# Attention and a mixture of experts on one core: softmax sums rearranged between engines, the first expert layer set inside an attention, weights requested later

## The chip, the cores and the metric

The kernel runs on one core of a Trainium2 chip. The metric is the device time of one execution in microseconds (us). A core has five engines that run their own instruction streams side by side: TensorE (PE, matmuls and, as PEld, weight loads), VectorE (DVE), ScalarE (ACT), GpSimd (POOL) and SyncE (SP, which here only starts DMA transfers). They wait for one another through semaphores. Matmul results land in PSUM, everything else lives in SBUF.

## What is computed

Grouped-query attention (8 batches, 16 query heads, 4 key heads, 384 positions, head size 64), then a mixture of experts with two gates (4 groups of 4 experts, 1024 by 1024 layers) on its output. Cut to what matters:

```python
scores = scale * np.matmul(q, k.transpose(0, 1, 3, 2))
attn = np.exp(scores - max); attn = attn / (sum + 1e-09)
x = np.matmul(attn, v)                      # (3072, 1024)
g_idx = argmax(x @ w_group)                 # group, then expert in it
e_idx = argmax(xg @ w_expert[g])
h = np.maximum(x[mask_e] @ w1[g, e], 0.0)
out[tok_idx] = g_w * e_w * (h @ w2[g, e])
```

## The kernel before

A batch is worked in two stages. Its **attention** (`Attn.run`) goes through 24 chunks u: four key groups g of six chunks c. For chunk u it issues the scores of chunk u+2 on TensorE (L292), their exp on ScalarE into a tile `e` of 128 x 768 (L298), and then the P·V product of chunk u (`pv`, L311), fp32, into a PSUM tile of its group. `tail` (L320) folds the six `e` tiles of a group into one with five adds on VectorE (L318), and at the end of a group moves the PSUM tile into `xT`, on ScalarE (L345), for group 1 of batches 2 to 7 on VectorE (L343). Tiles `e` come from a pool of twelve. `reduce_keys` (L366) sums the four folded tiles over keys with a transposing reduction (L370), `sums` (L375) adds partitions by small matmuls (L379) and takes the reciprocal (L382), `normalise` (L384) spreads it by a transpose (L389) and multiplies (L394), `cast` (L396) writes bf16 `xb` on ScalarE.

The **block** of batch b (`block`, L659) comes after its attention and does the expert of batch b-1: `moe_h` (64 matmuls and four ReLUs), then the three output products `ffn_y` and `y_out`, and between them the closing sums, normalise and the gate of batch b: `gate_logits` (L409), `gate_tokens` (L434), `guess_mean` (L423, evacuated by L426), `guess_logits` (L439), `gate_softmax`. The gate also guesses from a mean of v which expert most tokens of the next batch will take; `pick` reads its number into a register of GpSimd, and `pick_w1`/`pick_w2` request that expert's weights, 2 MB each in bf16, on GpSimd's DMA queue. A loop at the end does experts that were not guessed; here it is entered zero times.

Batches 0 and 1 are the start: attention 0 runs alone, with the transposes of its queries and keys between chunks; attention 1 has the closing sums, normalise and gate of batch 0 as `inserts` between its chunks; block 1 then does the expert of batch 0. The order of all this is written out by hand: each engine executes its instructions in the order of the code. K and q of batch b+2 are requested on GpSimd's queue, v on SP's; SP then transposes k and q of batch b+1 by DMA (`trans_k`, `trans_q`, L127, L119), with all outputs behind it in the same queue.

Of the kernel before, what the change touches and what calls it, by code (L numbers as in the profile page):

```python
# [18 lines left out]
def kernel(  # L19
# [28 lines left out]
    NB = S // 32  # L48
    scale = 1.0 / (D ** 0.5)
# [208 lines left out]
    def first_scores():  # L258
        new_kT(0)
        new_qT(0)  # L260
        warm = ps_tile("o")
        for i in range(8):
            nc.tensor.matmul(out=warm[:, i % 2, :], lhsT=onesb[:, :P], rhs=onesb, start=True,
                             stop=True)
# [3 lines left out]
        first_k(0, "s", nc.vector)  # L268
        first_q(0, SC, "s", nc.scalar)
        first_q(SC, SC, "o", nc.vector)  # L270
        nc.gpsimd.tensor_copy(out=k16[0][:, NC:NK].rearrange("p c d -> p (c d)"), in_=k0f[:, 1])
# [3 lines left out]
    xT, xb, ess = {}, {}, {}  # L275

    class Attn:
        def __init__(self, b):
            self.b = b
            self.e, self.oT = {}, {}  # L280
            ess[b] = {}
# [35 lines left out]
        def add(self, u, v_):  # L317
            nc.vector.tensor_add(out=self.e[u], in0=self.e[u], in1=self.e[v_])  # L318

        def tail(self, u):  # L320
# [3 lines left out]
            if c == 0 and g:  # L324
                self.add(z - NC, z - NC + 2)
            elif c in (1, 3):
                self.add(u - 1, u)
            elif c >= 4:
                self.add(z + 2 * (c - 4), u)
            if c == NC - 1:  # L330
                ess[b][g] = self.e[z]
                if g == Hkv - 1:
                    self.add(z, z + 2)
# [17 lines left out]
        def run(self, inserts, nxt=None):  # L351
            for u in range(NU):
# [11 lines left out]
    red, inv = {}, {}  # L364

    def reduce_keys(b, gs):  # L366
        if b not in red:
            red[b] = gpool.tile([P, Hkv, 2, NB], F32, name="red")
        for g in gs:
            nc.vector.tensor_reduce(  # L370
                out=red[b][:, g].rearrange("p t j -> p (t j)"),
                in_=ess[b][g].rearrange("p t (j x) -> p (t j) x", x=32),
                axis=AX.X, op=ALU.add, apply_transpose=True)

    def sums(b, which):  # L375
        sm = ps_tile(which, [P, Hkv, KG, NB])
        for r in range(2):
            for t in range(2):
                nc.tensor.matmul(out=sm[t * D:(t + 1) * D, :, r, :], lhsT=half32[:, r, :],  # L379
                                 rhs=red[b][:, :, t, :], start=True, stop=True)  # L380
        inv[b] = gpool.tile([P, KQ, NB], F32, name="inv")
        nc.vector.reciprocal(out=inv[b], in_=sm.rearrange("p g r j -> p (g r) j"))  # L382

    def normalise(b, m):  # L384
        if b not in xb:
            xb[b] = xpool.tile([P, KQ, S], BF16, name="xb")
        ks = slice(2 * m, 2 * m + 2)
# [28 lines left out]
    def guess_mean(b, pt):  # L416
# [9 lines left out]
        nc.vector.tensor_copy(out=vm, in_=pm)  # L426
# [15 lines left out]
    def gate_softmax(b, glp, guess):  # L442
# [5 lines left out]
        nc.vector.tensor_copy(out=gl, in_=glp[:, lo:hi])  # L448
# [54 lines left out]
    def pick(b):  # L503
# [13 lines left out]
        ers[b] = nc.gpsimd.value_load(e_i[0:1, 0:1], min_val=0, max_val=NE - 1)  # L517
# [83 lines left out]
    state = {}
# [17 lines left out]

    GB = KG * SC  # L620
    at[0].run({
        0: [gate_matrix_b],
        1: [do(first_q, GB, GB, "x", nc.vector)],
        3: [index_constants],
        5: [do(first_k, 1, "x", nc.vector)],
        7: [do(first_q, 2 * GB, GB, "x", nc.scalar)],
        12: [do(first_q, 3 * GB, GB, "x", nc.scalar)],
        18: [first_guess],
        20: [first_pick],
    }, at[1])  # L630
    load_v(2)
    load_k(2)
    load_q(2)

    def first_gate():
        state["pt"] = ps_tile("x")
        state["vm"] = guess_mean(1, state["pt"])
        gate_logits(0, state["pt"])

    def first_softmax():  # L640
        glp = gate_rows(state["pt"])
        gate_tokens(0, glp)
        guess_logits(state["vm"], glp)
        weights[0] = gate_softmax(0, glp, True)
        pick(1)
        pick_w2(1)

    weights = {}
    ins = {0: [do(reduce_keys, 0, range(Hkv))], 4: [do(sums, 0, "x")]}
    for i in range(4):  # L650
        ins.setdefault(5 + 2 * i, []).append(do(normalise, 0, i))
        ins.setdefault(7 + 2 * i, []).append(do(cast, 0, i))
    ins.setdefault(4, []).append(do(before_attention, 1))
    ins.setdefault(13, []).append(first_gate)
    ins.setdefault(15, []).append(first_softmax)
    at[1].run(ins)
    nc.sync.dma_start(out=xb_dram[0], in_=xb[0])

    def block(b):  # L659
        last = b == B - 1  # L660
        f = b - 1
        if b + 2 < B:
            load_v(b + 2)
            load_k(b + 2)
            load_q(b + 2)
        moe_h(f, 0, "s")
        reduce_keys(b, range(Hkv))
        weights[f]()
        out_weights(f)
        moe_h(f, 2, "s")  # L670
        sums(b, "o")
        for m in range(4):
            normalise(b, m)
        moe_h(f, 4, "s")
        moe_h(f, 6, "s")
        cast(b, 0)
        cast(b, 1)
        if b == 1:
            pick_w1(1)
        moe_y(f, 0, "s")  # L680
        cast(b, 2)
        cast(b, 3)
        nc.sync.dma_start(out=xb_dram[b], in_=xb[b])
        y = ffn_y(w2s[f], hTs[f], 1, "s", (0,))
        gate_logits(b, ps_tile("o"))
        ffn_y(w2s[f], hTs[f], 1, "s", (1,), y)
        y_out(f, 1, y)
        pt = ps_tile("s")
        glp = gate_rows(pt)
        vm = None if last else guess_mean(b + 1, pt)  # L690
        gate_tokens(b, glp)
        if not last:
            guess_logits(vm, glp)
        y = ffn_y(w2s[f], hTs[f], 2, "o", (0,))
        if not last:
# [3 lines left out]
        if not last:  # L699
            pick(b + 1)  # L700
            pick_w1(b + 1)
        ffn_y(w2s[f], hTs[f], 2, "o", (1,), y)
        if not last:
            pick_w2(b + 1)
# [119 lines left out]
```

## Time and profile before

| | us |
|---|---|
| median of 3 runs (401.49 to 401.89) | 401.64 |
| the profiled execution | 401.64 |
| its span, first to last instruction | 399.7 |
| busy: TensorE / VectorE / ScalarE / GpSimd | 372.5 / 293.4 / 241.7 / 29.7 |
| mean granted TensorE clock | 0.983 |

The 1.9 us between the execution and its span lie outside what the profile shows. A busy share says how long an engine had an instruction in hand, not what the kernel waited for; that is read from the stretches, waits and timelines below. A period of the steady part (one attention and one block) is 45.3 us, and six of them make up most of the span.

### The profile page before, as it was taken

The page shows a single profiled execution, that of the slowest core. Times are in us where ns is not written, and L with a number is a line of the kernel's source. Part 1 is how long each engine was busy: PE and PEld are TensorE (multiplying, and loading weights), DVE is VectorE, ACT ScalarE, POOL GpSimd, SP SyncE. Part 2 cuts the span into 40 slices and gives each one's busy share as a digit, 9 for nine tenths or more (in the row PEclk, how much of TensorE's full clock was granted, in tenths as well). Part 3 has the DMA queues.
Part 4 walks back from the last instruction along what each step waited for, and adds up shares of the span by engine and source line. Part 5 has one row for each costly group of instructions (what it writes and reads, how often), then busy time and mean ns, then how long its engine had stood idle before and what let it go on. Part 6 is the DMA issues. An engine that isn't in the chain of part 4 may idle for free.

```text
span 399.7 us, 8883 instructions
## 1 busy us (share of the span) xinstructions
PE 372.5 (93%) x3631; PEld 196.3 (49%) x3631; DVE 293.4 (73%) x502; ACT 241.7 (60%) x328; POOL 29.7 (7%) x45
## 2 busy tenths in 40 slices
PE   7999567999999999999999999999999999999992
PEld 3455133554555455554555455554555445554541
DVE  4678994993799649993799749993799748994230
ACT  4599373634892659744893559735894549735220
POOL 5001100200100020000100020000100001000000
PEclk9999798999999999999999999999999999999998
DMA  8972999999999999999999999999999999954424
GB/s 200 221 104 55 213 212 155 207 241 250 246 190 197 168 266 226 196 196 225 280 174 197 167 250 214 199 197 237 270 144 177 175 271 176 214 100 134 104 65 95
DMA packets 71209, 76.02 MB, mean 190 GB/s; under 512 B 35928, under 2 KB 50264, under 8 KB 71168
## 3 DMA queue, kind: packets, MB, share of 16 engines
q0 software_dynamic: 26640, 41.03, 60.0%
q1 hardware_dynamic: 44176, 33.94, 40.1%
q8 instruction: 29, 0.48, 0.5%
q10 hardware_dynamic: 352, 0.48, 0.4%
q14 instruction: 12, 0.10, 0.1%
HBM read 89.21 MB, written 18.87 MB: 270 GB/s over the span
## 4 chain that ended last, share of the span: by engine, by line
PE 63%; DVE 15%; ACT 12%; issue 7%; DMA 1%; ACTq 0%; DVEq 0%
PE ps_s L549 19%; PE ps_s L558 14%; PE ps_o L311 10%; DVE e L318 9%; ACT e L298 9%; PE ps_o L558 8%; PE ps_s L292 5%; PE ps_o L409 3%; ACT xT L345 2%; DVE red L370 2%; PE ps_s L434 1%; PE ps_o L549 1%; DMA w<-in_moe_w_expert_dram 1%; ACT ot L573 1%; DVE rb L389 1%
## 5 line engine op out<-in xcount | busy, mean ns | idle before, releaser
L298 ACT ACTIVATE e<-ps_s 128x768 f32<-128x768 f32 x192 | 146.4, 824 | 36.0 <-PE ps_s L292 35.4
L311 PE MATMUL ps_o<-e,v_raw 64*64 64x384 f32 x1536 | 158.2, 494 | 2.3 <-DVE inv L382 1.5
L318 DVE TENSOR_TENSOR e<-e 128x768 f32<-128x768 f32 x160 | 145.0, 953 | 20.0 <-PE ps_o L311 9.6
L549 PE MATMUL ps_s<-xb,w 128*128 128x384 bf16 x480 | 80.8, 326 | 0.0
L311 PEld LDWEIGHTS ps_o<-e,v_raw 64*64 64x64 f32 x1536 | 62.7, 136 | 26.7 <-issue 15.3
L292 PE MATMUL ps_s<-qT,kT 64*64 64x384 bf16 x768 | 68.8, 338 | 4.8 <-ACT e L298 2.7
L549 PEld LDWEIGHTS <-w 128*128 128x128 bf16 x512 | 48.9, 98 | 36.0 <-issue 4.2
L551 ACT ACTIVATE hT<-ps_s 128x768 bf16<-128x768 f32 x30 | 24.3, 811 | 58.7 <-PE ps_s L549 58.7
L292 PEld LDWEIGHTS <-kT 64*64 64x64 bf16 x768 | 32.0, 107 | 54.2 <-issue 49.8
L558 PEld LDWEIGHTS <-hT 128*128 128x128 bf16 x384 | 36.0, 98 | 45.2 <-issue 5.4
L558 PE MATMUL ps_s<-w,hT 128*128 128x512 bf16 x248 | 56.4, 379 | 0.0
L558 PE MATMUL ps_o<-w,hT 128*128 128x512 bf16 x136 | 32.0, 379 | 0.0
L389 DVE STREAM_TRANSPOSE rb<-inv 128x768 f32<-128x768 f32 x32 | 31.3, 977 | 1.0
L370 DVE TRANSPOSE_TENSOR_REDUCE red<-e 128x24 f32<-128x768 f32 x32 | 28.4, 944 | 0.0
L394 DVE TENSOR_TENSOR xT<-xT,rb 128x768 f32<-128x768 f32 x28 | 26.8, 958 | 1.4
L577 ACT ACTIVATE ot<-ps_s,we 128x1024 f32<-128x1024 f32 x14 | 15.6, 1114 | 17.6 <-PE ps_s L558 17.6
L398 ACT CAST xb<-xT 128x768 bf16<-128x768 f32 x28 | 22.0, 829 | 1.7 <-DVE xT L394 1.7
L345 ACT COPY xT<-ps_o 128x768 f32<-128x768 f32 x22 | 17.5, 797 | 6.6 <-PE ps_o L311 6.6
L426 DVE CAST vm<-ps_s 128x4 bf16<-128x4 f32 x6 | 1.0, 162 | 27.7 <-PE ps_s L423 27.7
L492 POOL DMA_DIRECT2D w<-in_moe_w_dram x8 | 7.0, 879 | 114.3 <-PE ps_s L292 64.1
L409 PE MATMUL ps_o<-xT,wg 128*32 128x384 f32 x112 | 11.3, 524 | 4.4 <-DVE vm L426 4.4
L91 POOL DMA_DIRECT2D k<-in_k_dram x7 | 4.9, 706 | 92.1 <-DMA kT<-k 92.1
(114 smaller groups left out, 164.5 us busy)
## 6 DMA issues: line engine op xcount, KB each, us to landing
w<-in_moe_w_dram POOLq DMA_DIRECT2D x16, 2048.0 KB, 24.7
out_dram<-ot SPq DMA_DIRECT2D x42, 256.0 KB, 6.2
xb_scratch<-xb SPq DMA_DIRECT2D x8, 768.0 KB, 9.0
q_raw<-in_q_dram POOLq DMA_DIRECT2D x7, 768.0 KB, 15.5
v_raw<-in_v_dram SPq DMA_DIRECT2D x14, 384.0 KB, 7.9
out_dram<-ot SPq DMA_DIRECT2D x12, 128.0 KB, 2.3
k<-in_k_dram POOLq DMA_DIRECT2D x7, 192.0 KB, 11.9
w<-in_q_dram POOLq DMA_DIRECT2D x3, 192.0 KB, 7.2
```

Of the source, the lines that this page charges most:

```text
L292: nc.tensor.matmul(out=sT[r * H2:(r + 1) * H2, s, :S], lhsT=kT[b][s * D:(s + 1) * D, slot, ks], rhs=qT[b][s * D:(s + 1) * D, kq * SC:(kq + ...
L298: nc.scalar.activation(e.rearrange("p t (s x) -> p s t x", s=2), sT[:, :, :S].rearrange("p s (t x) -> p s t x", t=2), ACT.Exp, scale=scale)
L311: nc.tensor.matmul(out=oT[t * D:(t + 1) * D, r, :S], lhsT=vraw[b][r * H2:(r + 1) * H2, g, c * D:(c + 1) * D], rhs=self.e[u][r * H2:(r + 1) ...
L318: nc.vector.tensor_add(out=self.e[u], in0=self.e[u], in1=self.e[v_])
L345: nc.scalar.copy(out=dst, in_=src)
L370: nc.vector.tensor_reduce(out=red[b][:, g].rearrange("p t j -> p (t j)"), in_=ess[b][g].rearrange("p t (j x) -> p (t j) x", x=32), axis=AX ...
L389: nc.vector.transpose(out=rb.rearrange("p k (j x) -> p (k j) x", x=32), in_=inv[b][:, ks].rearrange("p k j -> p (k j)").unsqueeze(2).to_br ...
L394: nc.vector.tensor_mul(out=x, in0=x, in1=rb)
L409: nc.tensor.matmul(out=lg[32 * t:32 * t + 32, :S], lhsT=wg[:, kq, :], rhs=xT[b][:, kq, :], start=(jj == 0), stop=(jj == KQ // 4 - 1))
L549: nc.tensor.matmul(out=h[:, jj, :S], lhsT=w1[:, kq, (f0 + jj) * P:(f0 + jj + 1) * P], rhs=x[:, kq, :], start=(kq == 0), stop=(kq == KQ - 1))
L551: nc.scalar.activation(hT[:, f0:f0 + 2, :], h[:, :, :S], ACT.Relu)
L558: nc.tensor.matmul(out=y[:, nh, :], lhsT=hT[:, f, c * P:(c + 1) * P], rhs=w2[:, f, nh * HALF:(nh + 1) * HALF], start=(f == 0), stop=(f == ...
```

## The change

What it does, part by part:

- **Sums.** `tail` adds only two pairs of `e` tiles per group, now on GpSimd; VectorE reduces four tiles per group with the transposing reduction, into `red` with four entries per group, and `collect` adds the four. The 20 adds and 4 reductions of a batch on VectorE become 8 adds on GpSimd, 16 reductions and a small reduction on VectorE. For batches 0 and 1 reductions can be held back (`hold`) and issued later (`release`).
- **Copies.** For batches 2 to 7 VectorE moves all four PSUM tiles into `xT`; ScalarE no longer does.
- **Start.** Eight more matmuls of ones (`fill`) around the first scores; the gate matrix is built in chunks 4 and 5 of attention 0; constants move ahead.
- **Batch 0's closing work.** `sums` and `normalise` in two halves, the first within attention 0; the products of batch 0 on GpSimd.
- **Attention 1** stops after chunk 13: there stand `moe_h` of batch 0 and batch 0's gate, and half of batch 1's normalise; then chunks 14 to 23. Block 1 keeps the output products.
- **Weights.** `pick` only reads the register. The weights are requested at the start of the next block, after `transposed`, a one-column copy on GpSimd that waits for the query transposes of the following batch. K, q and v of batch b+2 follow them.
- **Gate.** `guess_mean` comes after `gate_tokens`, and `guess_logits` after half of the third output product.

```diff
+        def add(self, eng, u):
+            eng.tensor_add(out=self.e[u], in0=self.e[u], in1=self.e[u + 1])
+
+        def reduce(self, g, n, u):
...
+                nc.vector.tensor_reduce(
+                    out=reds[self.b][:, g, n].rearrange("p t j -> p (t j)"),
+                    in_=self.e[u].rearrange("p t (j x) -> p (t j) x", x=32),
+                    axis=AX.X, op=ALU.add, apply_transpose=True)
+            if self.held is None:
+                emit()
+            else:
+                self.held.append(emit)
...
-            if c == 0 and g:
-                self.add(z - NC, z - NC + 2)
-            elif c in (1, 3):
-                self.add(u - 1, u)
-            elif c >= 4:
-                self.add(z + 2 * (c - 4), u)
+            if c in (1, 3):
+                self.add(nc.gpsimd, u - 1)
+            if c >= 3:
+                self.reduce(g, c - 3, (z, z + 4, z + 5)[c - 3])
             if c == NC - 1:
+                self.reduce(g, NR - 1, z + 2)
...
-                if g == 1 and b > 1:
+                if b > 1:
                     nc.vector.tensor_copy(out=dst, in_=src)
...
+    def collect(b, g0, g1):
+        nc.vector.tensor_reduce(
+            out=rsum[b][:, g0:g1].rearrange("p g t j -> p g (t j)"),
+            in_=reds[b][:, g0:g1].rearrange("p g n t j -> p g (t j) n"), axis=AX.X, op=ALU.add)
...
+    def scale_x(b, m, rb, eng):
+        eng.tensor_mul(out=x, in0=x, in1=rb)
...
+    def transposed(b):
+        nc.gpsimd.tensor_copy(out=after, in_=qT[b][:, KQ * SC - 1, :1])
+    def first_fetch():
+        pick(0)
+        transposed(1)
+        pick_w1(0)
+        pick_w2(0)
...
+        14: [do(hold, a), first_guess],
+        16: [first_pick, do(collect, 0, 0, 2), a.release],
+        19: [do(sums, 0, 0, 2, "x"), do(spread0, 0), do(spread0, 1)],
+        21: [first_fetch],
     }, at[1])
+    collect(0, 2, Hkv)
+    loads(2)
+    a = at[1]
+    hold(a)
+    a.run(0, 14, {
+        0: [do(scale0, 0)],
+        2: [do(scale0, 1)],
+        4: [do(cast, 0, 0)],
+        6: [do(sums, 0, 2, Hkv, "x"), do(spread0, 2), do(spread0, 3), do(scale0, 2), do(scale0, 3),
+            do(cast, 0, 1), a.release, do(transposes, 2)],
+        11: [do(cast, 0, 2)],
+        13: [do(cast, 0, 3)],
+    })
+    moe_h(0, 0, "s")
+    pt = ps_tile("x")
+    gate_logits(0, pt)
+    moe_h(0, 2, "s")
+    glp = gate_rows(pt)
+    gate_tokens(0, glp)
+    vm = guess_mean(1, pt)
+    moe_h(0, 4, "s")
+    guess_logits(vm, glp)
+    collect(1, 0, 2)
+    weights[0] = gate_softmax(0, glp, True)
+    pick_index(1)
+    pick(1)
+    moe_h(0, 6, "s")
+    sums(1, 0, 2, "x")
+    normalise(1, 0)
+    normalise(1, 1)
...
+    a.run(14, NU, {})
     def block(b):
+        if not last:
+            transposed(b + 1)
+        pick_w1(b)
+        pick_w2(b)
         if b + 2 < B:
+            loads(b + 2)
```

Three places in the instruction order. First, VectorE in attention 1, from the last sums of batch 0 on. `e` tiles are written in place, `rb` is the spread reciprocal. Before:

```order
L318 TENSOR_TENSOR e<-e 128x768 x4
L370 TENSOR_REDUCE red<-e 128x24 x4
L318 TENSOR_TENSOR e<-e 128x768 x3
L382 RECIPROCAL inv<-ps_o_681 128x96
L318 TENSOR_TENSOR e<-e 128x768
L389 STREAM_TRANSPOSE rb<-inv 128x768
L394 TENSOR_TENSOR xT<-xT,rb 128x768
L318 TENSOR_TENSOR e<-e 128x768 x2
L389 STREAM_TRANSPOSE rb<-inv 128x768
L394 TENSOR_TENSOR xT<-xT,rb 128x768
L318 TENSOR_TENSOR e<-e 128x768
L389 STREAM_TRANSPOSE rb<-inv 128x768
```

Of the change:

```order
L413 STREAM_TRANSPOSE rb<-inv 128x768 x2
L336 TENSOR_REDUCE red<-e 128x24 x4
L395 TENSOR_REDUCE rsum<-red 128x48
L407 RECIPROCAL inv<-ps_o_733 128x48
L413 STREAM_TRANSPOSE rb<-inv 128x768 x2
L336 TENSOR_REDUCE red<-e 128x24 x8
L240 CAST vm<-ps_o_864 128x4
L395 TENSOR_REDUCE rsum<-red 128x48
```

The adds, and the products between the transposes, are gone from VectorE; reductions stand there, those of held tiles among them, and a reciprocal in two parts.

Second, GpSimd around the first request for weights (`w_568`, `w_608` are w1 of batch 0; `e_i` is its register's source; ISA rows work out the address). Before, from the cast of k on:

```order
L271 CAST w_84<-w_84 128x384
L517 TENSOR_LOAD e_i
L517 ISA x2
L492 ISA
L492 DMA w_568<-in_moe_w_dram 128x8x1024
L498 ISA
L498 DMA w_570<-in_moe_w_dram 128x8x1024
L91 DMA k_613<-in_k_dram 128x2x384
L96 DMA q_raw<-in_q_dram 128x8x384
```

Of the change, from the cast of k on:

```order
L281 CAST w_84<-w_84 128x384
L329 TENSOR_TENSOR e<-e 128x768 x7
L554 TENSOR_LOAD e_i
L554 ISA x2
L643 COPY after<-qT 128x1
L524 ISA
L524 DMA w_608<-in_moe_w_dram 128x8x1024
L530 ISA
L530 DMA w_610<-in_moe_w_dram 128x8x1024
L92 DMA k_642<-in_k_dram 128x2x384
L97 DMA q_raw<-in_q_dram 128x8x384
L423 TENSOR_TENSOR xT<-xT,rb 128x768
```

Seven more adds stand ahead of the register load, the marker copy behind it, and the products of batch 0 (L423) behind four requests.

Third, VectorE in a steady attention (batch 2), from the product `ot` on. Before:

```order
L574 TENSOR_SCALAR ot<-ps_o_1201,we 128x512
L318 TENSOR_TENSOR e<-e 128x768 x8
L343 COPY xT<-ps_o_1365 128x768
L318 TENSOR_TENSOR e<-e 128x768 x11
L370 TENSOR_REDUCE red<-e 128x24 x4
L479 TENSOR_REDUCE smx<-ex 128x6
```

Of the change:

```order
L611 TENSOR_SCALAR ot<-ps_o_1223,we 128x512
L336 TENSOR_REDUCE red<-e 128x24 x4
L369 COPY xT<-ps_o_1312 128x768
L336 TENSOR_REDUCE red<-e 128x24 x4
L369 COPY xT<-ps_o_1393 128x768
L336 TENSOR_REDUCE red<-e 128x24 x4
L369 COPY xT<-ps_o_1467 128x768
L336 TENSOR_REDUCE red<-e 128x24 x4
L369 COPY xT<-ps_o_1541 128x768
L395 TENSOR_REDUCE rsum<-red 128x96
```

The adds give way to four reductions a group, and each group has its copy out of PSUM.

## Rows read from the trace of the kernel before

**Rows 1.** Stretches of the span: busy us of each engine (instructions), granted clock, DMA share, GB/s.
```profile
35.90:75.30 39.40, 27.90 (x330) 12.95 (x322) 33.66 (x57) 23.29 (x33) 4.95 (x6) 0.87 1.05 184
...
191.50:212.00 20.50, 20.16 (x285) 11.38 (x285) 17.76 (x21) 18.98 (x26) 1.76 (x2) 1.00 1.15 222
```

**Rows 2.** VectorE's groups by line, 35.9 to 62 us: count, busy us, mean ns, idle before.
```profile
L318 DVE TENSOR_TENSOR e<-e 128x768 f32<-128x768 f32 x15 | 13.6, 945 | 0.0
L389 DVE STREAM_TRANSPOSE rb<-inv 128x768 f32<-128x768 f32 x4 | 3.9, 969 | 0.0
L394 DVE TENSOR_TENSOR xT<-xT,rb 128x768 f32<-128x768 f32 x4 | 3.8, 958 | 0.1
```

**Rows 3.** TensorE's timeline, 34 to 102 us: start, us, instruction, count, idle before.
```profile
61.52 2.33 PE L409 MATMUL ps_o<-xT,wg 128*32 128x384 f32 x16 [4.41 <-DVE vm L426]
...
87.05 5.34 PE L558 MATMUL ps_s<-w,hT 128*128 128x512 bf16 x24
...
100.98 0.52 PE L292 MATMUL ps_s<-qT,kT 64*64 64x384 bf16 x8
```

**Rows 4.** A short stretch after that wait (columns as in rows 1).
```profile
62.00:64.00 2.00, 2.00 (x20) 0.43 (x12) 0.00 (x0) 0.10 (x1) 0.00 (x0) 0.51 1.31 204
```

**Rows 5.** Timeline of all engines in a steady attention, 188 to 236 us.
```profile
191.55 0.52 PE L292 MATMUL ps_s<-qT,kT 64*64 64x384 bf16 x8
...
193.62 0.36 PE L292 MATMUL ps_s<-qT,kT 64*64 64x384 bf16 x4
...
194.05 0.70 ACT L573 ACTIVATE ot<-ps_o,we 128x512 f32<-128x512 f32 x1
...
194.43 0.36 PE L292 MATMUL ps_s<-qT,kT 64*64 64x384 bf16 x4
...
195.50 0.36 PE L292 MATMUL ps_s<-qT,kT 64*64 64x384 bf16 x4
...
198.16 9.36 ACT L298 ACTIVATE e<-ps_s 128x768 f32<-128x768 f32 x12
```

**Rows 6.** TensorE's waits: engine, line, waited for, total us, times, longest.
```profile
PE ps_s L434 <- DVE vm L426: 2.1, 6, 0.3
```

**Rows 7.** TensorE's timeline at the start of the program.
```profile
1.60 3.60 PE L263 MATMUL ps_o<-onesb 128*128 128x512 bf16 x8 [1.60 <-DVE onesb L148]
...
9.24 1.54 PE L311 MATMUL ps_o<-e,v_raw 64*64 64x384 f32 x8
```

**Rows 8.** GpSimd's timeline: two casts, and the first request for weights.
```profile
1.52 0.28 POOL L160 CAST id128b<-id128f 128x128 bf16<-128x128 f32 x1
...
12.75 0.50 POOL L271 CAST w<-w 128x384 bf16<-128x384 f32 x1 [6.36 <-DMA w<-in_k_dram]
...
38.20 0.89 POOL L492 DMA_DIRECT2D w<-in_moe_w_dram  x1 [24.94 <-DVE e L318]
```

**Rows 9.** VectorE's timeline: first and last row of a softmax, and four transposing sums.
```profile
33.59 0.18 DVE L448 COPY gl<-ps_o 128x20 f32<-128x20 f32 x1 [0.91 <-PE ps_o L439]
...
36.52 0.15 DVE L516 CAST e_i<-ef 128x1 int32<-128x1 f32 x1
...
77.87 3.55 DVE L370 TRANSPOSE_TENSOR_REDUCE red<-e 128x24 f32<-128x768 f32 x4
```

**Rows 10.** TensorE's groups by line, 75.3 to 101 us.
```profile
L549 PE MATMUL ps_s<-xb,w 128*128 128x384 bf16 x64 | 10.7, 326 | 0.0
...
L409 PE MATMUL ps_o<-w,wg 128*32 128x384 f32 x16 | 1.5, 492 | 0.0
```

**Rows 11.** DMA issues at 38 to 41 us: count, KB each, us to landing.
```profile
w<-in_moe_w_dram POOLq DMA_DIRECT2D x1, 2048.0 KB, 14.8
...
q_raw<-in_q_dram POOLq DMA_DIRECT2D x1, 768.0 KB, 27.3
```

**Rows 12.** Queues of SP and GpSimd: k's copy ahead of the transposes, and the next q load.
```profile
63.80 0.52 SPq L125 DMA_DIRECT2D k<-k  x1
...
75.65 0.90 POOL L96 DMA_DIRECT2D q_raw<-in_q_dram  x1 [1.37 <-DMA qT<-q_raw]
```

More of the change, by code (lines that the diff above doesn't have):

```diff
@@ L261, in first_scores, with fill @@
         warm = ps_tile("o")
-        for i in range(8):
-            nc.tensor.matmul(out=warm[:, i % 2, :], lhsT=onesb[:, :P], rhs=onesb, start=True,
-                             stop=True)
+        def fill(n):
+            for i in range(n):
+                nc.tensor.matmul(out=warm[:, i % 2, :], lhsT=onesb[:, :P], rhs=onesb, start=True,
+                                 stop=True)
+        fill(8)
         nc.vector.tensor_copy(out=k16[0][:, :NC].rearrange("p c d -> p (c d)"), in_=k0f[:, 0])
@@ L360, in run, with sums @@
                     f()
[L364 to L375, printed above, removed]
+    rsum, inv = {}, {}
+    def collect(b, g0, g1):
+        if b not in rsum:
+            rsum[b] = gpool.tile([P, Hkv, 2, NB], F32, name="rsum")
+        nc.vector.tensor_reduce(
+            out=rsum[b][:, g0:g1].rearrange("p g t j -> p g (t j)"),
+            in_=reds[b][:, g0:g1].rearrange("p g n t j -> p g (t j) n"), axis=AX.X, op=ALU.add)
+    def sums(b, g0, g1, which):
         sm = ps_tile(which, [P, Hkv, KG, NB])
@@ L640, in first_softmax @@
[L640 to L653, printed above, removed]
@@ L661, in block @@
         f = b - 1
+        if not last:
+            transposed(b + 1)
+        pick_w1(b)
+        pick_w2(b)
         if b + 2 < B:
[L663 to L686, printed above, removed]
+            loads(b + 2)
+        if b > 1:
+            moe_h(f, 0, "s")
+            collect(b, 0, Hkv)
+            weights[f]()
+            out_weights(f)
+            moe_h(f, 2, "s")
+            sums(b, 0, Hkv, "o")
+            for m in range(4):
+                normalise(b, m)
+            moe_h(f, 4, "s")
+            moe_h(f, 6, "s")
+            cast(b, 0)
+            cast(b, 1)
+            moe_y(f, 0, "s")
+            cast(b, 2)
+            cast(b, 3)
+            nc.sync.dma_start(out=xb_dram[b], in_=xb[b])
+            y = ffn_y(w2s[f], hTs[f], 1, "s", (0,))
+            gate_logits(b, ps_tile("o"))
+            ffn_y(w2s[f], hTs[f], 1, "s", (1,), y)
+        else:
+            collect(b, 2, Hkv)
+            y = ffn_y(w2s[f], hTs[f], 0, "s", (0,))
+            sums(b, 2, Hkv, "o")
+            for m in range(2, 4):
+                normalise(b, m)
+            cast(b, 0)
+            cast(b, 1)
+            ffn_y(w2s[f], hTs[f], 0, "s", (1,), y)
+            y_out(f, 0, y)
+            y = ffn_y(w2s[f], hTs[f], 1, "s")
+            cast(b, 2)
+            gate_logits(b, ps_tile("o"))
+            cast(b, 3)
+            nc.sync.dma_start(out=xb_dram[b], in_=xb[b])
         y_out(f, 1, y)
@@ L713 @@
         if b > 1:
-            before_attention(b)
-            at[b].run({1: [late]})
+            if b + 1 < B:
+                transposes(b + 1)
+            at[b].run(0, NU, {1: [late]})
         late = block(b)
```

141 lines of the change are left out of this document (80 added, 61 removed).

## The prediction

> **What bounds the kernel now.** I began with the table of stretches. In attention 1 (35.9 to 75.3 us) TensorE is busy 27.9 of 39.4 us at a mean granted clock of 0.87, while VectorE is busy 33.7; in a steady attention (191.5 to 212.0) TensorE is busy 20.16 of 20.5 [rows 1]. So the early part waits for VectorE and the rest is TensorE's own time. The groups of VectorE for 35.9 to 62 us show what it does there: 15 adds on tiles e at 0.945 us, the four transposes and four products of normalise at about 0.96, with 0.1 us of idle time before all of them [rows 2]. TensorE's timeline shows the price: the gate's logits start at 61.52 after 4.41 us of waiting behind normalise [rows 3]. Work after such a wait runs slowly: in 62 to 64 us the granted clock is 0.51, the lower of the two levels (1.2 of 2.4 GHz) [rows 4], and the logits take 2.33 us.
>
> In steady attention one chunk takes 0.81 us of TensorE (193.62 to 194.43). Where ScalarE puts another operation between two exps (the ot product at 194.05), the next chunk starts 1.07 us later [rows 5]: 0.26 lost, and as much at each copy into xT within a batch. The second scores of a batch stand at 100.98 and, two batches on, at 191.55 [rows 3, 5]: a period of 45.3. ScalarE's exps take 0.78 each (12 in 9.36 us), so it has no room for such extras without a slip. Last, the view of waits has six waits of TensorE in L434 for the small cast vm, 2.1 us together [rows 6].
>
> **The change, part by part.** The profiled execution took 401.64 us, the median of the runs, of which 399.7 is the span; all below is subtracted from 401.64.
>
> *Start.* Eight fill matmuls come in around the first scores; eight such took 3.60 us, 0.45 each [rows 7], and four of them stand before the first scores: up to 1.8 us lost, less what the gate matrix took there. On the other side, the first eight P·V matmuls took 1.54 us [rows 7], where a whole chunk takes 0.81 later; if the fills bring the higher clock three chunks earlier, 3 x 0.73 = 2.2 us come back. I take the middle of these bounds, 0.4 gained with the gate matrix off that place.
>
> *Pair adds on GpSimd.* No row shows a two-input operation on GpSimd. One-input casts take 0.28 us at 128 columns and 0.50 at 384 [rows 8]: 0.86 ns a column and 0.17 fixed, so 0.83 at 768 columns. That is the lower bound. With two inputs read in turn it is 1.5, with a third pass for the result 2.15, the upper bound. I take 1.5, as the casts show one pass for a read and its write. The Trainium skill, GPSIMD Engine Reference, section 3.1, has 4497 ns for a 2048-column add and 2.6 cycles an element for two inputs, which gives an estimate of 1.7 at 768 columns; by it the sum below would be about 1 us longer. Per group of six chunks (4.86 us) GpSimd then has 3.0 us of adds, VectorE four transposing sums of 0.89 (four in 3.55 [rows 9]) and, from batch 2 on, a copy as long as an add: 4.5 us. Both fit, VectorE barely. An e tile returns after twelve chunks, two groups, so such lateness reaches nobody.
>
> *Steady attentions (batches 2 to 7).* Three copies into xT leave ScalarE; two of them fell between exps of their batch. 6 x 2 x 0.28 = 3.3 us gained; the ot slip stays. VectorE's four closing sums (3.55 us) go, but TensorE did not wait for them there. The mean's evacuation now lies under the first half of the third output product, so the six waits of rows 6 go: 2.1 us.
>
> *Attention 1.* Count from the end of attention 0 (T, 35.9 us before). GpSimd's queue has, in order: the last add (20,21), ready at T-1.6 and done by T-0.1; the register load (before, from the end of e_i at 36.67 to the weight request at 38.20: 1.5 [rows 8, 9]); the marker that waits for the query transposes; four DMA requests of 0.88; then the first product of batch 0's normalise, at T+4.8 to 6.3. Behind it add, product, add, product, product: the last ends at T+13.8. ScalarE has come to its first cast at T+4.5 and waits 1.9 us for that product; behind the cast stand the exps, so TensorE stops too, at about T+5.8. After that ScalarE is the bound: 14 exps, 3 copies and 4 casts before the expert layer, 21 x 0.78 + 1.9 = 18.3. So the layer starts at T+18.3; w1, asked for at T+1.4, lands 14.8 us later [rows 11], T+16.2: in time by 2 us. Layer and logits take 10.7 and 1.5 [rows 10], the small products and the new sums together another 1.7 (an estimate: about as long as the logits), in all 13.9; the ten chunks left 8.1: T+40.3.
>
> *The new wait.* Ten chunks are not long enough for VectorE. The gate's softmax begins about 10.8 us after the layer and takes 3.1 (33.59 to 36.67, sixteen rows of about 0.2 [rows 9]): T+32.2. In its queue follow half of batch 1's normalise (two transposes, two products and a small reciprocal, 4.4), seven small operations of 0.2 (1.5), and eight sums that attention's second half left (7.1): T+45.2. TensorE wants the sums after one half of an output product, at T+42.0, and so waits 3.3 us; the work behind loses some 1.5 at the lower clock (after the wait in rows 3 the logits alone lost 2.33 - 1.5 = 0.8). What is left of block 1 took 13.9 us before (87.05 to 100.98 [rows 3]). In sum T + 40.3 + 13.9 + 0.4 + 3.3 + 1.5 = T+59.4, against 100.98 - 35.9 = 65.1 before: 5.7 gained.
>
> *Weights a block later.* The marker keeps the 4 MB of weights away from the transposes. From w1's request to q's landing is three requests of 0.88 and 27.3 = 30 us [rows 8, 11]; the output and xb copies add about 7 by their share of the bytes (3 MB beside 5), the transposes, until they hand back q's buffer, 11.9 (63.80 to 75.65 [rows 12]), of which 4 lie beside q's load. One round is about 45 us, give or take 2, against a period of 45.3 - 5.4/6 = 44.4. The first round is early: w1 of batch 1, asked for at T+41, lands by T+61 and is needed at T+59.4 + 20 = T+79. With 17 us in hand, five rounds of up to 3 us too much cost nothing.
>
> Sum: 401.6 - 0.4 - 5.7 - 3.3 - 2.1 = **390.1 us**.
>
> **The rivals.** (a) *Ports.* VectorE's two products in the resumed attention 1 read two SBUF operands while GpSimd adds. If each has to wait for an add of 1.5, the new wait grows by 3 us: 393.1. Rows 2 have VectorE's products beside an idle GpSimd, so the trace says nothing for or against. The Trainium skill, SBUF — State Buffer, section Who interferes with whom, states exactly this contention, and exempts the reductions. Chance 0.14.
>
> (b) *The gain of attention 1 goes into new waits.* If GpSimd takes 2.15, its product chain ends 3.9 us later, and if the clock falls at the cast's stop as in rows 4, another 2: 396 us or somewhat more. For it speaks that six of its operations stand in one queue behind four DMA requests. Chance 0.12.
>
> (c) *GpSimd bounds all attentions.* It decides from 2.43 us an add (two adds in 4.86). At 2.8, 8 adds take 22.4 instead of 19.4 us: 3.0 x 8 attentions, from 390.1 + 9 (b's chain) to 423. Against it: the casts' slope. Chance 0.06, slower.
>
> (d) *The DMA round bounds.* The chain is now closed: weights, then k and q, then their transposes, then the marker. It decides from 44.4 + 17/5 = 47.8 us a round. A round of 52 would lose 7.6 a batch; less the 17 in hand, five rounds cost 21: 411. For it: the DMA share stands above 1.0 in both stretches of rows 1. Against it: the round's sum of about 45. Chance 0.06, slower.
>
> (e) *It does nothing measurable*: after the stop at the cast the clock stays at the lower level into the expert layer, and 11 us of matmul work at half speed give back what attention 1 gained and more: 401. Chance 0.04.
>
> **How the numbers follow.** Forecast 386.5 to 394: 0.52; better than that (no new wait behind the expert layer, clock up early): 0.06, down to 383.5; (a) reaching to 397: 0.14; (b) 0.12; (c) and (d) 0.06 each; (e) 0.04. Range 383.5 to 399.5 leaves out (c), (d), (e) and the end of (b). A measurement of this kernel tells about 0.2% from no change: faster 0.84, same 0.04, slower 0.12.
>
> **What would show it.** The adds' row on GpSimd should read 1.4 to 1.8 us, over 2.43 makes (c) true. Attention 1 with the layer in it should end near 76 us and its ScalarE show one wait of 2 to 4 us for GpSimd before a cast. Block 1 should show TensorE waiting 2 to 5 us for the collecting sum. The steady period should shrink from 45.3 to about 44.3, with steps of 0.81 except at ot. Transposes of q should take far less than 20 us, and no matmul should wait for a weight DMA. The prediction is wrong if VectorE's row of sums is longer than 0.95 beside GpSimd, if the first expert layer waits for w1, or if steady batches grow.

## The result and the profile after

The changed kernel takes 392.77 us (median of 4 runs, 392.49 to 393.46) beside 401.76 us for the kernel before on the same chip (4 runs, 401.49 to 403.39). The ratio is 0.9771, with a 95% interval of 0.9742 to 0.98. The forecast was 390.1 us, so the direction was right and the gain was 9.0 us instead of 11.5. The profiled execution took 392.49 us with a span of 390.9; before they were 401.64 and 399.7.

The page of the changed kernel, busy time of each engine (share of the span, instructions), and GpSimd's group of adds further down:

```profile
PE 366.0 (94%) x3655; PEld 195.1 (50%) x3655; DVE 257.7 (66%) x462; ACT 233.6 (60%) x312; POOL 154.7 (40%) x120
...
L329 POOL TENSOR_TENSOR e<-e 128x768 f32<-128x768 f32 x64 | 116.4, 1837 | 172.1 <-ACT e L309 105.6
```

An add on GpSimd takes 1.84 us, where 1.5 was taken from bounds of 0.83 to 2.15. The table of stretches for attention 1 and for one steady attention answers to [rows 1]:

```profile
36.70:74.80 38.10, 33.80 (x402) 18.58 (x394) 25.96 (x44) 26.31 (x37) 24.67 (x16) 1.00 1.06 190
187.20:207.70 20.50, 20.27 (x289) 11.61 (x289) 17.28 (x27) 18.36 (x25) 14.44 (x8) 1.00 1.11 199
```

The columns are those of [rows 1]: stretch, its length, busy us of PE, PEld, VectorE, ScalarE and GpSimd, granted clock, DMA share, GB/s. Attention 1 now holds the expert's first layer (64 matmuls) and still takes 38.1 us, at a granted clock of 1.00, where it took 39.4 at 0.87 without it. What remains of waiting is seen in the view of TensorE's waits (line of the waiter, what it waited for, us in total, times, longest):

```profile
PE ps_o L403 <- DVE rsum L395: 9.8, 2, 7.2
PE ps_s L586 <- DMA w<-in_moe_w_dram: 2.2, 1, 2.2
PE ps_s L303 <- ACT e L309: 1.7, 7, 0.7
```

The six waits of [rows 6] are gone, and so is the one of 4.41 us of [rows 3]. Two new ones are for the collecting sum (`rsum`, 2.63 and 7.15 us), and one is for the expert weights w1. TensorE's timeline shows where they lie:

```profile
33.07 0.42 PE L403 MATMUL ps_o<-rsum,half 128*64 128x24 f32 x8 [2.63 <-DVE rsum L395]
...
53.35 2.77 PE L586 MATMUL ps_s<-xb,w 128*128 128x384 bf16 x16 [2.20 <-DMA w<-in_moe_w_dram]
...
74.84 1.90 PE L595 MATMUL ps_s<-w,hT 128*128 128x512 bf16 x8
83.90 0.63 PE L403 MATMUL ps_o<-rsum,half 128*64 128x24 f32 x8 [7.15 <-DVE rsum L395]
84.46 8.09 PE L595 MATMUL ps_s<-w,hT 128*128 128x512 bf16 x24
...
98.83 0.52 PE L303 MATMUL ps_s<-qT,kT 64*64 64x384 bf16 x8
...
187.22 0.52 PE L303 MATMUL ps_s<-qT,kT 64*64 64x384 bf16 x8
...
190.16 0.36 PE L303 MATMUL ps_s<-qT,kT 64*64 64x384 bf16 x4
...
191.23 0.36 PE L303 MATMUL ps_s<-qT,kT 64*64 64x384 bf16 x4
...
192.04 0.36 PE L303 MATMUL ps_s<-qT,kT 64*64 64x384 bf16 x4
```

The second scores of batch 2 stand at 98.83 us against 100.98 [rows 3], so the whole early part gained only 2.15 us. They stand at 187.22 two batches on: the period is 44.20 instead of 45.28, and from 188.55 on the steps between chunks are 0.81 except at ot (190.16 to 191.23). From batch 2 to the end of the span the kernel gained 298.72 - 292.07 = 6.65 us. So the loss against the forecast lies in the early part, above all in the 7.15 us at 83.90. The 24 matmuls behind that wait took 8.09 us, where 24 such took 5.34 before [rows 3], and the stretch that holds them has a mean granted clock of 0.65:

```profile
84.46:92.50 8.04, 8.04 (x30) 2.97 (x28) 4.24 (x5) 1.83 (x2) 0.00 (x0) 0.65 1.12 212
```

VectorE's timeline ahead of the wait shows why it is so long, together with GpSimd's:

```profile
67.65 0.98 DVE L413 STREAM_TRANSPOSE rb<-inv 128x768 f32<-128x768 f32 x1
68.66 2.04 DVE L423 TENSOR_TENSOR w<-w,rb 128x768 f32<-128x768 f32 x1
70.63 0.96 DVE L413 STREAM_TRANSPOSE rb<-inv 128x768 f32<-128x768 f32 x1
71.63 2.17 DVE L423 TENSOR_TENSOR w<-w,rb 128x768 f32<-128x768 f32 x1
...
73.93 1.57 DVE L513 TENSOR_TENSOR wt<-smx 128x3 f32<-128x3 f32 x1
...
76.35 6.98 DVE L336 TRANSPOSE_TENSOR_REDUCE red<-e 128x24 f32<-128x768 f32 x8
83.36 0.48 DVE L395 TENSOR_REDUCE rsum<-red 128x48 f32<-128x192 f32 x1
```

```profile
68.06 1.83 POOL L329 TENSOR_TENSOR e<-e 128x768 f32<-128x768 f32 x1 [12.17 <-ACT e L309]
71.16 4.32 POOL L329 TENSOR_TENSOR e<-e 128x768 f32<-128x768 f32 x2 [1.27 <-PE ps_s L303]
```

The first product starts at 68.66 inside an add (68.06 to 69.89) and ends 0.8 us behind it. The second ends 0.8 us behind the first of the next two adds, and the second of these adds comes late (4.32 us for the two, 1.84 is the mean of one); then a product of three columns, wt, takes 1.57 us, until that add has ended at 75.48. Transposes beside the same adds take 0.96 to 0.98 as ever. Elsewhere the same products take 0.96 [rows 2].

### The profile page after: what moved, and what is told of

It reads as the page before. It is cut to its first block, busy times and chain, and to the rows that moved or that the text cites. A ratio compares the mean times of both kernels' runs of the same rounds, so it can differ in the third digit from the quotient of the medians.

```text
span 390.9 us, 8899 instructions
## 1 busy us (share of the span) xinstructions
PE 366.0 (94%) x3655; PEld 195.1 (50%) x3655; DVE 257.7 (66%) x462; ACT 233.6 (60%) x312; POOL 154.7 (40%) x120
## 4 chain that ended last, share of the span: by engine, by line
PE 79%; DVE 7%; ACT 5%; DMA 4%; issue 2%; POOLq 0%; POOL 0%; ACTq 0%
PE ps_o L322 22%; PE ps_s L586 20%; PE ps_s L595 14%; PE ps_o L595 8%; PE ps_s L303 7%; DMA w<-in_moe_w_dram 4%; ACT e L309 4%; PE ps_o L441 3%; DVE red L336 2%; PE ps_o L266 1%; PE ps_o L586 1%; DVE w L423 1%; ACT ot L610 1%; PE ps_s L466 1%; PE ps_o L403 1%
## 5 line engine op out<-in xcount | busy, mean ns | idle before, releaser
L329 POOL TENSOR_TENSOR e<-e 128x768 f32<-128x768 f32 x64 | 116.4, 1837 | 172.1 <-ACT e L309 105.6
L309 ACT ACTIVATE e<-ps_s 128x768 f32<-128x768 f32 x192 | 149.1, 816 | 21.2 <-PE ps_s L303 18.4
L322 PE MATMUL ps_o<-e,v_raw 64*64 64x384 f32 x1536 | 153.5, 482 | 0.0
L336 DVE TRANSPOSE_TENSOR_REDUCE red<-e 128x24 f32<-128x768 f32 x128 | 113.4, 944 | 8.9 <-POOL e L329 8.6
L595 PE MATMUL ps_s<-w,hT 128*128 128x512 bf16 x248 | 59.1, 393 | 0.0
L303 PEld LDWEIGHTS <-kT 64*64 64x64 bf16 x768 | 29.4, 104 | 40.3 <-issue 37.0
L423 DVE TENSOR_TENSOR xT<-xT,rb 128x768 f32<-128x768 f32 x24 | 23.0, 958 | 0.8
L369 DVE COPY xT<-ps_o 128x768 f32<-128x768 f32 x24 | 22.0, 918 | 0.0
L403 PE MATMUL ps_o<-rsum,half 128*64 128x48 f32 (+1 forms) x80 | 4.5, 233 | 11.0 <-DVE rsum L395 9.8
L611 DVE TENSOR_SCALAR ot<-ps_o,we 128x512 f32<-128x512 f32 x7 | 5.3, 751 | 13.3 <-ACT ot L610 13.3
```

The costliest lines, as they stand in the source:

```text
L303: nc.tensor.matmul(out=sT[r * H2:(r + 1) * H2, s, :S], lhsT=kT[b][s * D:(s + 1) * D, slot, ks], rhs=qT[b][s * D:(s + 1) * D, kq * SC:(kq + ...
L309: nc.scalar.activation(e.rearrange("p t (s x) -> p s t x", s=2), sT[:, :, :S].rearrange("p s (t x) -> p s t x", t=2), ACT.Exp, scale=scale)
L322: nc.tensor.matmul(out=oT[t * D:(t + 1) * D, r, :S], lhsT=vraw[b][r * H2:(r + 1) * H2, g, c * D:(c + 1) * D], rhs=self.e[u][r * H2:(r + 1) ...
L329: eng.tensor_add(out=self.e[u], in0=self.e[u], in1=self.e[u + 1])
L336: nc.vector.tensor_reduce(out=reds[self.b][:, g, n].rearrange("p t j -> p (t j)"), in_=self.e[u].rearrange("p t (j x) -> p (t j) x", x=32) ...
L423: eng.tensor_mul(out=x, in0=x, in1=rb)
```

## The experiments

Theory P is that VectorE's operations with two operands in SBUF stand still while GpSimd adds. Rival Q is that VectorE's queue is simply too long there. Each ratio below is to the kernel before, run beside that experiment; the changed kernel's own is 0.9771 (0.9742 to 0.98).

**Without three adds** (their work is left out, so batch 1's closing sums miss rows):

```
-            if c in (1, 3):
+            if c in (1, 3) and not (b == 1 and u >= 14):
```

> Leaves out three of GpSimd's pair adds, those after chunks 15, 19 and 21 of attention 1, so batch 1's closing sums miss some rows; VectorE's queue is the same. Theory P (VectorE's two-operand operations stand still while GpSimd adds): the two products of batch 1's normalise take 0.96 us instead of 2.04 and 2.17, the small product wt 0.16 instead of 1.57, and TensorE's wait of 7.15 us for the collecting sum at the head of block 1 falls by about 3.7 to 3.4; with the clock behind it some 4 to 5 us in all: 388.5. Rival Q (VectorE has too many operations queued, whatever GpSimd does): the products keep their 2 us, the wait stays between 6.5 and 7.2, the time between 392 and 393.

Measured: 390.46 us, ratio 0.9723 (0.9628 to 0.9818). VectorE's and TensorE's timelines of this run:

```profile
70.98 0.96 DVE L423 TENSOR_TENSOR w<-w,rb 128x768 f32<-128x768 f32 x1
...
72.86 0.96 DVE L423 TENSOR_TENSOR w<-w,rb 128x768 f32<-128x768 f32 x1
...
73.94 0.16 DVE L513 TENSOR_TENSOR wt<-smx 128x3 f32<-128x3 f32 x1
```

```profile
53.99 4.46 PE L586 MATMUL ps_s<-xb,w 128*128 128x384 bf16 x16 [2.07 <-DMA w<-in_moe_w_dram]
...
82.51 0.63 PE L403 MATMUL ps_o<-rsum,half 128*64 128x24 f32 x8 [3.44 <-DVE rsum L395]
83.07 8.20 PE L595 MATMUL ps_s<-w,hT 128*128 128x512 bf16 x24
```

P is shown by the rows: with the adds gone and the queue the same, the products take 0.96, wt 0.16, and the wait is 3.44 where 3.4 was expected. The total shows nothing by itself, since its interval covers the changed kernel's. It moved less than expected for two reasons that the trace has: the first part of the layer took 4.46 us instead of 2.77 in this execution, and the work behind a wait of 3.44 ran as slowly as behind 7.15 (8.20 us).

**Two products on GpSimd**, behind its last add:

```
-    normalise(1, 0)
-    normalise(1, 1)
+    rbs[0] = spread(1, 0)
+    rbs[1] = spread(1, 1)
...
     a.run(14, NU, {})
+    scale_x(1, 0, rbs[0], nc.gpsimd)
+    scale_x(1, 1, rbs[1], nc.gpsimd)
```

> The first two products of batch 1's normalise go from VectorE to GpSimd, behind its last add of attention 1 (75.5); their transposes stay on VectorE. P: VectorE loses 2.04 and 2.17 from its queue ahead of the held-over sums, so the wait at the head of block 1 falls by 4.2, to about 2.9, and with the clock behind it 5 us are gained: 387.7. Q: only the 0.96 that a product costs by itself goes, twice, the wait falls to about 5.2, the time to 390.5. The products on GpSimd end by 79.5, ahead of the casts that read them.

Measured: 385.72 us, ratio 0.9633 (0.9557 to 0.9709). TensorE's timeline, and the stretch of the 24 matmuls:

```profile
79.84 0.42 PE L403 MATMUL ps_o<-rsum,half 128*64 128x24 f32 x8 [1.57 <-DVE rsum L395]
80.19 5.35 PE L595 MATMUL ps_s<-w,hT 128*128 128x512 bf16 x24
...
91.83 0.52 PE L303 MATMUL ps_s<-qT,kT 64*64 64x384 bf16 x8
```

```profile
80.20:85.50 5.30, 5.30 (x31) 2.28 (x28) 4.24 (x5) 2.36 (x3) 3.13 (x4) 1.00 1.13 190
```

The wait fell by 5.6 us, more than P's 4.2 and Q's 1.9, since wt was freed too (0.32 us). The 24 matmuls behind it took 5.35 us instead of 8.09, at a granted clock of 1.00 instead of 0.65. The second scores of batch 2 came 7.0 us earlier, and the time followed. The clock loss went only here, where the products' own 0.96 us each left the queue along with the hold; without the adds it had stayed. Over all runs these 24 matmuls took 5.35 us behind waits of 0.41 to 2.26 us and 7.02 to 8.22 behind waits of 3.44 to 7.16; so the time lost at the lower clock did not grow in step with the wait.

**The collecting sum ahead of the softmax chain**, alone and with the products on GpSimd:

```
-        16: [first_pick, do(collect, 0, 0, 2), a.release],
+        16: [do(collect, 0, 0, 2), first_pick, a.release],
```

> The collecting sum of groups 0 and 1 of batch 0 stands ahead of the first softmax chain on VectorE, nothing else moves. P and Q alike: TensorE's wait of 2.63 us at 33.1 goes, since the sum has its data by 28. What it is worth tells two others apart. If the start was lost to that wait alone, attention 0 ends 2.6 us earlier, at 34.1, and the time is 390.2. If the request for w1 (36.5) keeps its place, since the chain of the first choice sets it, the layer in attention 1 waits for w1 longer by as much (2.20 now, 4 to 5 then) and the time stays within 0.5 of 392.8.

> Both edits: the collecting sum ahead of the first softmax chain, and the two products on GpSimd. P: the two gains add up, 385 to 386.5 (less if the layer in attention 1 then waits for w1: 387.5). Q: 388 to 390.5.

Measured: 392.86 us, ratio 0.9811 (0.9737 to 0.9885), and 386.12 us, ratio 0.9658 (0.9578 to 0.9738): no gain, and none beside the products alone. The expected reason was a longer wait for w1, but in neither trace does TensorE wait for w1. The trace of the first shows another, in TensorE's and VectorE's timelines:

```profile
30.96 0.42 PE L403 MATMUL ps_o<-rsum,half 128*64 128x24 f32 x8
...
38.62 1.56 PE L322 MATMUL ps_o<-e,v_raw 64*64 64x384 f32 x8 [3.72 <-DVE inv L407]
```

```profile
30.55 1.71 DVE L540 SCALAR_TENSOR_TENSOR key<-oh_first,eback 128x16 f32<-128x16 bf16 x1
...
32.50 1.85 DVE L544 TENSOR_SCALAR oh_all<-key,km 128x16 f32<-128x16 f32 x1
...
34.67 3.55 DVE L336 TRANSPOSE_TENSOR_REDUCE red<-e 128x24 f32<-128x768 f32 x4
38.14 0.42 DVE L407 RECIPROCAL inv<-ps_o 128x48 f32<-128x48 f32 x1
```

The sums come without a wait. But their PSUM buffer is the one that the next attention's P V matmuls need, and the reciprocal that reads it stands behind four released reductions, so the wait of 2.63 us comes back as one of 3.72. Two small operations of the chain take 1.71 and 1.85 us and end when the adds beside them on GpSimd end (0.17 and 0.23 elsewhere).

**Copies back on ScalarE** (`if g == 1 and b > 1:` again ahead of the copy on VectorE):

> Three of the four copies into xT of batches 2 to 7 go back from VectorE to ScalarE, where they stood before. The prediction's term: two of them a batch fall between exps and cost 0.28 us each, 3.3 us over six batches: 396.1, the period from one batch's second scores to the same two batches on 45.3 / 44.2 apart by 0.55 a batch, and two more steps of about 1.07 us between chunks of an attention. Rival: ScalarE has slack enough since the mean's evacuation left TensorE's path, and the copies cost nothing: within 0.5 of 392.8, steps of 0.81 all through.

Measured: 396.58 us, ratio 0.9885 (0.9847 to 0.9922). The second scores of batches 2, 3 and 7 stand at 98.90, 143.72 and 322.97: a period of 44.81, 0.61 more a batch, 3.7 us over six. The attention of batch 4 has two more long steps between chunks, of 1.12 and 1.11 us, as the term said. The term of 3.3 holds, with 0.3 a copy.

**The guess's logits at once** (as before, the guess's mean ahead of `gate_tokens` and its logits right behind, then the output product, for batches 2 on):

```
+        vm = None if last else guess_mean(b + 1, pt)
         if b > 1:
             gate_tokens(b, glp)
-        vm = None if last else guess_mean(b + 1, pt)
+            if not last:
+                guess_logits(vm, glp)
...
         if b == 1:
             gate_tokens(b, glp)
+            guess_logits(vm, glp)
         if not last:
-            guess_logits(vm, glp)
```

> The guess's logits follow the mean's evacuation at once, as before, instead of half an output product later. The prediction's term: six waits of TensorE for vm of 0.3 us come back, 2.1 us: 394.9. Rival: the wait is paid back in full by an earlier softmax, since the choice of the next expert then starts earlier: within 0.5 of 392.8.

Measured: 396.38 us, ratio 0.9877 (0.9841 to 0.9913), with a period of 44.78. TensorE's timeline at the end of a block:

```profile
273.88 0.82 PE L466 MATMUL ps_s<-mod,lgs 128*128 128x20 f32 x6 [0.35 <-DVE vm L240]
```

The wait of 0.35 is back, and the period grows by 0.58 a batch, 3.5 us in all, where the waits alone gave 2.1. The term was the right one and too small. The other 0.23 a batch has no row of waiting; part of it is that the six matmuls behind the wait take 0.82 us, where they take 0.74 in the changed kernel.

**No extra fills** (the eight matmuls left out, a tile that nobody reads):

> The eight extra fill matmuls are left out (they write a tile that nobody reads). The prediction's term: 0.4 us lost without them, between 1.8 gained (their own time) and 2.2 lost (first P V groups at the lower clock, 1.54 us where 0.81 are usual). By the trace of the changed kernel the whole start with them, up to the scores after chunk 19, is 2.1 us earlier than before, so the fills may carry all of that: 392.8 + 0.4 to 392.8 + 2.2. Rival: what they gain is lost again in the wait of 2.63 us at 33.1, which ends when VectorE's chain ends: the wait gets shorter by what the start gets longer, and the time stays within 0.4 of 392.8.

Measured: 394.42 us, ratio 0.9832 (0.9799 to 0.9865). The start is not where it lost:

```profile
8.44 0.84 PE L320 MATMUL ps_o<-e,v_raw 64*64 64x384 f32 x8
...
32.83 0.42 PE L401 MATMUL ps_o<-rsum,half 128*64 128x24 f32 x8 [2.62 <-DVE rsum L393]
...
53.80 4.45 PE L584 MATMUL ps_s<-xb,w 128*128 128x384 bf16 x16 [2.25 <-DMA w<-in_moe_w_dram]
```

Without fills the first P V group takes 0.84 us (0.82 with them) and the sums come 0.24 us earlier. The loss of 1.9 us (second scores of batch 2 at 100.70) is mostly the first part of the layer behind the w1 wait, 4.45 us instead of 2.77. Both readings fell: the fills gain nothing at the start. The same slow first part appears in two other runs (4.46 and 4.22) and not in six (2.77), after waits of 2.0 to 2.7 us, so whether the fills have a part in it stays open.

**Weights asked for early**, and **no marker**. In the first, w1 and w2 of batches 2 on are asked for behind the choice at the end of the block, as before, and without the marker; its edit is shown below. In the second only the marker is left out, and the requests keep the new place.

```
-        if not last:
+        if b == 1:
             transposed(b + 1)
-        pick_w1(b)
-        pick_w2(b)
+            pick_w1(b)
+            pick_w2(b)
...
             pick(b + 1)
+            pick_w1(b + 1)
...
+            pick_w2(b + 1)
```

> From batch 2 on w1 and w2 are asked for as before, right behind the choice at the end of the block, without the marker that waits for the query transposes; batch 1 keeps its place. The prediction's term: nothing, since TensorE waited for no transpose before and waits for no weight after; the transposes of q take 20 us and more each again instead of about 4: 392.8, give or take 0.5. Rival: the late request is what keeps the round of transfers near the batch period (44 to 46 us of 44.2), and the early one gains slack but no time; or transposes that take 20 us now come too late for the faster attention: 1 to 4 us slower, with TensorE's scores waiting for qT.

> Only the marker is left out: w1 and w2 are asked for at the head of the block as in the changed kernel, but without waiting for the query transposes. Two readings of the run with the early weights (404.35) differ here. Queue: there TensorE lost time because the requests for k, q, w1 and w2 stood, waiting, ahead of the next attention's pair adds in GpSimd's queue, so that four adds came together 4 to 8 us late; here the same requests wait inside the block, which has 24 us and no adds, so the time stays within 1 of 392.8 though transposes take 20 us again. Transposes: weights beside the transposes cost the time themselves, as the scores need qT: then 2 to 10 us slower here too, with TensorE waiting for qT.

Measured: 404.35 us, ratio 1.0051 (1.0015 to 1.0086), half a per cent slower than the kernel before; and 393.22 us, ratio 0.9783 (0.9743 to 0.9824), no difference from the changed kernel. The early weights in one batch, in GpSimd's, VectorE's and TensorE's timelines:

```profile
234.30 0.89 POOL L97 DMA_DIRECT2D q_raw<-in_q_dram  x1 [14.03 <-DMA qT<-q_raw]
244.53 0.87 POOL L524 DMA_DIRECT2D w<-in_moe_w_dram  x1 [9.34 <-PE ps_s L303]
245.50 0.87 POOL L530 DMA_DIRECT2D w<-in_moe_w_dram  x1
246.39 7.14 POOL L329 TENSOR_TENSOR e<-e 128x768 f32<-128x768 f32 x4
...
248.25 3.56 DVE L336 TRANSPOSE_TENSOR_REDUCE red<-e 128x24 f32<-128x768 f32 x4 [4.36 <-POOL e L329]
251.73 0.92 DVE L369 COPY xT<-ps_o 128x768 f32<-128x768 f32 x1
...
252.70 0.88 PE L322 MATMUL ps_o<-e,v_raw 64*64 64x384 f32 x8 [2.02 <-DVE xT L369]
```

Requests that wait stand in front of the adds. The attention began at 239.85 (second scores); its first four adds come together at 246.39, VectorE's reductions wait 4.36 us for them, the copy that frees the PSUM buffer comes late, and TensorE waits 2.02 us and then slows down (mean granted clock 0.57 from 253.5 to 257.5). This batch took 48.15 us instead of 44.20. The one before it took 50.27, with a wait of 0.95 us for such a copy at 201.36 and one of 2.48 at 209.55 for which the trace names no releaser. In the kernel before the same requests waited on a GpSimd that had no adds. What held w1 from the register's source (241.2) to 244.53 the trace does not show. Query transposes, duration minimum, median and maximum in ns, with the early weights and without the marker:

```profile
L120 SPq DMA_TRANSPOSE qT<-q_raw x6: 4191/24002/27552, 70.0 to 294.6; - x6
```

```profile
L120 SPq DMA_TRANSPOSE qT<-q_raw x6: 3707/4154/4326, 70.6 to 293.7; - x6
```

In the changed kernel the median is 3932, in the kernel before 24545. The place of the request alone keeps weights and transposes apart; the marker adds nothing. Since the transposes are short without the marker too, that run does not tell the two readings apart, the queue and slow transposes. The trace of the early weights speaks for the queue: TensorE waits 3.8 us in four waits for copies out of PSUM there, and 1.49 us in one, at 143.26, for a query transpose.

**Better versions.** One puts batch 0's five small weight operations behind the collecting sum, with the products on GpSimd. The next adds the early collecting sum, with the held reductions released only behind the reciprocal, and the layer behind chunk 16:

```
-    weights[0]()
-    out_weights(0)
...
             collect(b, 2, Hkv)
+            weights[f]()
+            out_weights(f)
...
-        16: [first_pick, do(collect, 0, 0, 2), a.release],
-        19: [do(sums, 0, 0, 2, "x"), do(spread0, 0), do(spread0, 1)],
+        16: [do(collect, 0, 0, 2), first_pick],
+        19: [do(sums, 0, 0, 2, "x"), do(spread0, 0), do(spread0, 1), a.release],
...
-    a.run(0, 14, {
+    a.run(0, 17, {
```

> The two products on GpSimd as in the run of them alone (385.7), and the five small operations for batch 0's weights (1.35 us of VectorE) behind the held-over sums and the collecting sum instead of ahead. By P the wait at the head of block 1 (1.57 us there) falls to about 0.2: 384.3. Rival: the output products of batch 0 need these weights and their evacuation comes late, nothing is gained: 385.7.

> As the run before, and: the collecting sum of batch 0 ahead of the first softmax chain with the held-over sums released only behind the reciprocal (so that the buffer of the sums comes free in time), and the first expert layer three chunks later, behind chunk 16. The wait of 2.63 us goes, attention 0 ends about 2 us earlier, and three chunks (2.4 us) lie in the time in which w1 was waited for: 2.4 us less than the run before, 382. Rival: GpSimd's chain of products and adds (it ended at 50.6) or the new place of the reciprocal (the next group's P V needs its buffer one chunk after the layer) takes the gain back: 384 to 386.

Measured: 384.81 us, ratio 0.9594 (0.9555 to 0.9632), with a wait of 0.41 at the head of block 1; and 383.38 us, ratio 0.9546 (0.951 to 0.9582), the lowest of all, though the two intervals overlap. In the latter the wait for w1 is gone and 0.28 us is left of the one in attention 0; parts come back in attention 1 (2.31 us for the collecting sum, and waits for exps) and at the head of block 1 (0.85):

```profile
PE ps_o L403 <- DVE rsum L395: 3.2, 2, 2.3
PE ps_s L303 <- ACT e L309: 3.1, 8, 1.1
```

## Why the prediction was right, and where its sizes were off

The total came out nearer than its parts. Up to the second scores of batch 2 the change gained 2.15 us where 6.1 were forecast; behind them it gained 1.25 more than forecast, and 0.35 outside the span. That these partly cancel is luck.

**The new wait** is the term that was mis-sized: 3.3 us of waiting (3.2 by the prediction's own times) and 1.5 at the lower clock were predicted, and 7.15 and 2.74 (8.09 against 5.35) were measured, 5.1 us more. Its queue was listed rightly, with VectorE's operations at the price they have beside an idle GpSimd. Rival (a) had the mechanism, 3 us for the two products, and 393.1 as its time; the runs without adds and with the products moved show it, with 2.3 us for the two products and 1.4 more for wt, which nobody had counted. The loss at the lower clock was too small by itself: without the adds the wait was 3.44 us, near the forecast, and the 24 matmuls behind it still lost 2.85 (8.20 against 5.35). Rival (a) was given a chance of 0.14. That the measured 392.77 is so near its 393.1 is luck too, since the other parts are each off by more than that. The Trainium skill, SBUF — State Buffer, section Who interferes with whom, says that a VectorE instruction with two SBUF inputs contends with a GpSimd instruction that reads SBUF, and that one with at most one SBUF input, outside VectorE's two-port performance modes, doesn't; the transposes and reductions here (0.96 and 0.88 beside adds) and the products (2.04 and 2.17) agree.

**Start.** 0.4 gained was predicted (the sum of its bounds, 1.8 lost and 2.2 gained; their middle is 0.2); attention 0 ended at 36.67, 0.74 later than before. The part up to chunk 19 was 2.1 us faster (29.63 for its P V group against 31.74), without any help of the fills (29.39 in the run without them). Nor is it shown that the first P V groups were slow for the clock: the trace of the kernel before has a granted clock of 1.00 from 8 to 13 us. The gate matrix, which moved too, was not tested apart. Then TensorE waited 2.63 for the collecting sum, which stands behind a softmax chain on VectorE that an add lengthened by 1.5.

**Attention 1 and the layer** took 38.2 us from the end of attention 0 where 40.3 was predicted. ScalarE waited 0.8 us for GpSimd's products instead of 1.9, because the register load, taken as 1.5, cost nothing (GpSimd's add ends at 36.42, w1 is asked for at 36.49). The margin of 2 us for w1 was not there: w1 took 16.8 us to land instead of 14.8, and TensorE, done with its chunks at 51.15, waited 2.2 us for it. By the prediction's own last sentence this is a sign that it was wrong; the other two (longer sums beside GpSimd, longer batches) did not come. The wait is worth less than it looks: ScalarE's last cast for the layer ends at 53.93, and where nothing waited for w1 (the two runs with the early collecting sum) the layer's first 16 matmuls waited 1.6 us for ScalarE instead. Rivals (b) and (e) did not occur: the granted clock of attention 1 is 1.00. Beside holding VectorE, the add's 1.84 us instead of 1.5 shows in one wait of ScalarE, 0.47 us at 52.40.

**Copies and the guess's logits.** 5.4 us were predicted and 6.65 measured. (The prediction reads 0.26 a copy and reckons with 0.28.) Undone one by one they cost 3.7 and 3.5 us by the periods, 1.19 a batch together where the period gained 1.08; what gives back that 0.1 stays open.

**Weights a block later** was costed at nothing, with the marker as what protects the transposes. Against the kernel before that is what one sees, but it is no free edit: with the adds on GpSimd, the old place costs about 11 us (404.35 against 392.77, and a ratio of 1.0051 against 0.9771). The prediction had looked at the round of transfers and not at what stands behind a waiting request in GpSimd's queue. The round itself was right, 44 to 46 us between requests, and rivals (c) and (d) did not occur.

## What to carry to other kernels

Before work is moved to GpSimd, list which two-operand operations VectorE has in the same stretch, however small they are: here each took 1.1 to 1.5 us more while GpSimd added, and moving two of them along was worth 7 us, beside 9.0 for the whole change. An engine that issues DMAs must not get work that the path needs behind requests that can wait. When a wait is taken away, look who next needs the buffer that was waited for: here the wait went from the sums (2.63 us) to the P V matmuls (3.72).

## What the hardware showed unexpectedly

The hold did not go by the size of VectorE's operation: 128x3 took 1.57 us instead of 0.16, 128x16 1.70 instead of 0.17. A comparison of 16 columns with one value per partition (L544) was held too, 1.85 instead of 0.23, though it has one tensor input; so theory P, with its two operands, does not name all that was held. GpSimd is held in turn (two adds in 4.32 us instead of 3.62).

After a wait of 2.0 to 2.7 us for w1 the next 16 matmuls took 2.77 us in six executions and 4.2 to 4.5 in three. The waits were 2.16 to 2.66 us in the six and 2.03, 2.07 and 2.25 in the three, so a longer wait does not make the difference. The rows have a mean granted clock of 1.00 in the changed kernel from 53.3 to 66.7 us and of 0.88 from 54 to 68 in the run without fills. No run shows what decides it.
